# Loading the first pair early by hardware queues, and row tiles in batch 1, in a fused attention and feed-forward kernel

## Chip, cores and metric

One core of one Trainium2 chip. The metric is the time of one execution on the device, in microseconds (us); lower is better. Most executions of this kernel agree within 0.3%; the profiler's span, from the first to the last instruction, is some 2 us shorter than the time of the same run. The clock records of these traces show TensorE's clock as granted in two steps: full, or half. Where a run's mean granted clock is given, 0.99 in a span of 350 us means about 7 us at half clock.

## The reference

```python
def _attn_ref(q, k, v, f):                 # 8 batches, 8 heads, 576 tokens, head size 64; fp32
    scores = scale * np.matmul(q, k.transpose(0, 1, 3, 2))
    log_f = np.log(np.clip(f, 0.0001, 1.0))
    cum = np.cumsum(log_f, axis=-1)
    decay = cum[:, :, :, None] - cum[:, :, None, :]
    scores = np.where(causal, -1000000000.0, scores + decay)
    attn = np.exp(scores - np.max(scores, axis=-1, keepdims=True))
    attn = attn / (np.sum(attn, axis=-1, keepdims=True) + 1e-09)
    return np.matmul(attn, v)

def _moe_ref(x, w_in, w_out):              # 4608 tokens, 512 -> 2048 -> 512
    h = x @ w_in
    g = 0.5 * h * (1.0 + erf(h / sqrt(2)))
    return g @ w_out
# reference: x = attention, heads side by side; result = _moe_ref(x, w_in, w_out)
```

The decay is a ratio of exponentials, so the kernel does not add it to the scores: it weighs v (and a column of ones beside it) with exp(-cum) and divides by the weighed sum.

## The kernel before

Names: a *pair* is two heads, of which a batch has four; a *score tile* is one of four groups (t = 0 to 3) of a pair's scores; *AV* is the product of the exponentials with the weighed v, one per head; GEMM1 and GEMM2 are the two halves of the feed-forward. From batch 1 on, matmuls of GEMM2 of the batch before are put between the score tiles (*fills*). A GEMM2 step `"n"` is one full 128-row matmul; `"r"` is two *row tiles* of 64 rows that run beside each other into two PSUM banks, whose contents VectorE adds.

The start: loads, then the work on VectorE and ScalarE, then TensorE's order.

```python
    f_sb = consts.tile([BH, S], FP32)
    nc.sync.dma_start(f_sb, f.rearrange("b h s -> (b h) s"))
    load_qk_tokens(0, 0, 2)          # GpSimd queue: fp32 in memory, bf16 in SBUF
    load_qk_tokens(0, 2, 4)
    ident_bf = consts.tile([P, P], BF16)
    make_identity(nc, ident_bf)
    load_qk_tokens(0, 4, 6)
    nc.gpsimd.memset(v_sb[:, :, 0, 0:1], 0.0)
    load_v(0, 0, 4)
    ...                              # the masks key_of and after, on GpSimd
    nc.vector.tensor_scalar(f_sb, f_sb, 1e-4, 1.0, Alu.max, Alu.min)
    nc.scalar.activation(lf, f_sb, Act.Ln)
    nc.vector.memset(v_sb[0:D, :, 4, :], 0.0)
    nc.vector.tensor_tensor_scan(cum, ones, lf, 0.0, Alu.mult, Alu.add)
    nc.scalar.activation(wk, cum, Act.Exp, bias=cum[:, S // 2 : S // 2 + 1], scale=-1.0)
    ...
        warm_up(11)                  # matmuls on zeros
        transposes(0, o_psum, "o")   # q copied out by ScalarE, k by VectorE
        nc.vector.tensor_copy(key_of[D:P], key_of[0:D])
        nc.vector.tensor_copy(after[D:P], after[0:D])
        warm_up(2)
        scores(0, 0, 0)              # each ends in an exp on ScalarE
        scores(0, 0, 1)
        transposes(1, m_psum, "m")
        scores(0, 0, 2)
        ...                          # wk transposed to wT, which weighs v
```

Batch 1, and the plan of GEMM2 under batches 3 to 7:

```python
        for i in range(HP):          # pairs
            for t in range(4):
                scores(b, i, t)
                ...
                take(fill, FILL_1[i][t])          # 2 fills a tile in pairs 2 and 3
                if i and t in (1, 2):
                    av(i - 1, t - 1)
                if i > 1 and t == 0:
                    to_xT(b, i - 2, nc.vector.tensor_copy, o_psum, "o")
        to_xT(b, HP - 2, nc.vector.tensor_copy, o_psum, "o")
        av(HP - 1, 0)
        av(HP - 1, 1)
        gemm1_begin(1, both)

    PLAN = [
        (0, "o", 16 * "r"),
        (1, "m", 6 * "r" + "n" + 9 * "r"),
        (2, "m", "n" + 9 * "r" + "n" + 5 * "r"),
        (3, "s", 7 * "r" + 9 * "n"),
    ]
```

The softmax here doesn't subtract the row's maximum and nothing guards it: scores larger than these inputs give would overflow.

## Time and profile before

| | before |
|---|---|
| time, median | 348.35 us |
| span of the profiled run (its time: 347.52 us) | 345.7 us |
| TensorE busy | 95% |
| first score exp / first AV / first score of batch 1 | 8.60 / 17.12 / 39.67 us |
| batch 1 / batch 2 / each of batches 3 to 6 | 32.60 / 46.91 / 36.16 us |

A stage is read from the timeline, as the distance between the first instructions of two kinds. A timeline line gives start, duration, engine, source line, operation, output and inputs, shape and how many instructions were put together; in brackets how long the engine stood still before it, and what ended that.

### The profile page before, as it was taken

The page shows a single profiled execution, that of the slowest core. Times are in us where ns is not written, and L with a number is a line of the kernel's source. Part 1 is how long each engine was busy: PE and PEld are TensorE (multiplying, and loading weights), DVE is VectorE, ACT ScalarE, POOL GpSimd, SP SyncE. Part 2 cuts the span into 40 slices and gives each one's busy share as a digit, 9 for nine tenths or more (in the row PEclk, how much of TensorE's full clock was granted, in tenths as well). Part 3 has the DMA queues.
Part 4 walks back from the last instruction along what each step waited for, and adds up shares of the span by engine and source line. Part 5 has one row for each costly group of instructions (what it writes and reads, how often), then busy time and mean ns, then how long its engine had stood idle before and what let it go on. Part 6 is the DMA issues. An engine that isn't in the chain of part 4 may idle for free.

```text
span 345.7 us, 7895 instructions
## 1 busy us (share of the span) xinstructions
PE 328.3 (95%) x3187; PEld 173.7 (50%) x3227; DVE 188.1 (54%) x424; ACT 212.1 (61%) x296; POOL 125.1 (36%) x256
## 2 busy tenths in 40 slices
PE   7899999999999999999899989998999899999995
PEld 3674555445554455545554555445544554444443
DVE  5670456934367935795479647974597542020011
ACT  5976786773634787368746874687468765503600
POOL 8390673128418044533345333624261430000000
PEclk9999999999999999999999999999999999999999
DMA  8999999979992999488935995498900230011013
GB/s 116 176 171 194 202 178 147 170 149 161 222 183 100 138 202 176 81 119 167 219 89 81 134 211 137 74 161 190 170 30 2 69 83 30 2 61 61 0 35 89
DMA packets 99924, 43.03 MB, mean 124 GB/s; under 512 B 78704, under 2 KB 95344, under 8 KB 99888
## 3 DMA queue, kind: packets, MB, share of 16 engines
q1 hardware_dynamic: 82592, 28.37, 42.4%
q0 software_dynamic: 16896, 13.63, 26.9%
q8 instruction: 25, 0.41, 0.5%
q10 hardware_dynamic: 400, 0.52, 0.4%
q14 instruction: 11, 0.09, 0.1%
HBM read 36.85 MB, written 9.44 MB: 134 GB/s over the span
## 4 chain that ended last, share of the span: by engine, by line
PE 89%; DVE 4%; ACT 3%; issue 2%; POOL 2%; POOLq 0%; ACTq 0%; DVEq 0%
PE ps L375 35%; PE ps L466 25%; PE o L320 9%; PE ps L408 8%; PE s L289 8%; ACT e L299 2%; PE ps L501 2%; PE ps_x L353 1%; DVE ot L474 1%; PE ps_f L206 1%; DVE x L334 1%; POOL q L107 1%; POOL k L107 1%; DVE qT L213 0%; DVE kT L213 0%
## 5 line engine op out<-in xcount | busy, mean ns | idle before, releaser
L392 ACT ACTIVATE g<-ps 128x512 bf16<-128x512 f32 x144 | 85.3, 597 | 80.2 <-PE ps L375 80.2
L299 ACT ACTIVATE e<-s 128x896 bf16<-128x896 f32 (+2 forms) x128 | 101.0, 836 | 32.1 <-PE s L289 28.2
L375 PE MATMUL ps<-xT,w_in_sb 128*128 128x512 bf16 x497 | 111.4, 379 | 0.8
L466 PE MATMUL ps<-w_out_sb,g 64*128 64x512 bf16 (+1 forms) x736 | 104.0, 376 | 4.7 <-DVE ot L474 3.9
L375 PEld LDWEIGHTS <-w_in_sb 128*128 128x128 bf16 x576 | 56.0, 98 | 67.5 <-issue 1.8
L301 POOL TENSOR_SCALAR_AFFINE_SELECT e<-e 128x256 bf16<-128x256 bf16 (+1 forms) x135 | 49.5, 385 | 100.1 <-ACT e L299 99.9
L466 PEld LDWEIGHTS <-g 64*128 64x128 bf16 (+1 forms) x756 | 39.8, 94 | 40.4 <-issue 10.6
L244 DVE COPY qT<-tq 64x288 bf16<-64x288 bf16 x96 | 49.3, 514 | 1.4
L260 POOL TENSOR_TENSOR vw<-v_sb,wT 128x640 bf16<-128x640 f32 x31 | 39.6, 1279 | 24.7 <-DMA v_sb<-in_v_dram 24.5
L289 PE MATMUL s<-qT,kT 64*128 64x320 bf16 (+4 forms) x384 | 43.9, 277 | 3.3 <-ACT e L299 2.6
L320 PE MATMUL o<-vw,e 128*128 128x65 bf16 x960 | 36.8, 194 | 2.7 <-issue 2.4
L320 PEld LDWEIGHTS <-e 128*128 128x128 bf16 x960 | 34.8, 98 | 9.2 <-POOL e L301 4.1
L474 DVE COPY ot<-ps 128x512 f32<-128x512 f32 x26 | 17.9, 690 | 35.5 <-PE ps L466 35.5
L244 DVE COPY kT<-tk 64x288 bf16<-64x288 bf16 x96 | 33.0, 344 | 1.6
L334 DVE TENSOR_TENSOR x<-o,r 128x320 bf16<-128x320 f32 x64 | 31.5, 492 | 2.2
L417 DVE COPY ot<-ps 128x512 f32<-128x512 f32 (+2 forms) x9 | 5.7, 632 | 48.8 <-PE ps L408 31.9
L289 PEld LDWEIGHTS <-kT 64*128 64x128 bf16 x384 | 18.7, 94 | 22.6 <-issue 7.3
L333 DVE RECIPROCAL r<-o 128x5 f32<-128x5 f32 x64 | 12.2, 190 | 30.8 <-PE o L320 30.7
L408 PE MATMUL ps<-w_out_sb,g 128*128 128x512 bf16 (+2 forms) x142 | 27.9, 355 | 0.1
L408 PEld LDWEIGHTS <-g 128*128 128x128 bf16 x144 | 13.5, 98 | 14.5
L476 DVE TENSOR_TENSOR ot<-ot,ps 128x512 f32<-128x512 f32 x26 | 17.9, 687 | 1.2
L375 PE MATMUL ps<-tails,w_in_sb 128*128 128x512 bf16 x63 | 14.3, 377 | 0.1
(64 smaller groups left out, 148.2 us busy)
## 6 DMA issues: line engine op xcount, KB each, us to landing
out_dram<-ot SPq DMA_DIRECT2D x32, 256.0 KB, 2.3
v_sb<-in_v_dram SPq DMA_DIRECT2D x24, 256.0 KB, 5.7
q<-in_q_dram POOLq DMA_DIRECT2D x6, 576.0 KB, 6.2
k<-in_k_dram POOLq DMA_DIRECT2D x6, 576.0 KB, 8.2
v_sb<-in_v_dram SPq DMA_DIRECT2D x22, 128.0 KB, 5.3
w_in_sb<-in_moe_w_in_dram POOLq DMA_DIRECT2D x4, 512.0 KB, 7.0
w_out_sb<-in_moe_w_out_dram POOLq DMA_DIRECT2D x4, 512.0 KB, 8.4
q<-in_q_dram POOLq DMA_DIRECT2D x4, 144.0 KB, 4.5
```

Of the source, the lines that this page charges most:

```text
L244: nc.vector.tensor_copy(rows[:, odd], src[odd * D : (odd + 1) * D, 2 * i + h].rearrange("d j p -> d p j"),)
L260: eng.tensor_tensor(vw_of[b][:, hs, :, 0:D], v_sb[:, hs, :, :], w.unsqueeze(3).to_broadcast([P, 2, NBLK, D]), Alu.mult,)
L289: nc.tensor.matmul(to, *ab, start=half < 0, stop=half == 1 or not masked)
L299: nc.scalar.activation(et[:, :, z:c], st[:, :, z:c], Act.Exp, scale=scale)
L301: nc.gpsimd.affine_select(out=et[:, :, c0 + z : c0 + P], in_=et[:, :, c0 + z : c0 + P], compare_op=Alu.is_ge, fill=0.0, base=z, pattern=[[ ...
L320: nc.tensor.matmul(o[:, m, :], e_of[b, i, t][:, h, c : c + P], vw_of[b][:, 2 * i + h, n, :], start=(n == 0), stop=(n == m),)
L334: nc.vector.tensor_tensor(x_of[b, i][:, :, h, :], o[:, :, 0:D], r.unsqueeze(2).to_broadcast([P, NBLK, D]), Alu.mult,)
L375: nc.tensor.matmul(ps, w_in_sb[:, kt, ffb * P : (ffb + 1) * P], src[:, kt, 0:TC], start=(kt == 0), stop=(kt == n_dm - 1),)
L392: nc.scalar.activation(g_of[c][ffb], ps, Act.Gelu)
L408: nc.tensor.matmul(pss[ts][:, c0:c1], g_of[c][kt][:, ts * P : (ts + 1) * P], w_out_sb[:, kt, c0:c1], start=(kt == 0), stop=(kt == n_ff - 1),)
L466: nc.tensor.matmul(banks[r], g_of[c][kt][rows, ts * P : (ts + 1) * P], w_out_sb[rows, kt, :], start=kt == (steps.index("r") if r else 0), ...
L474: nc.vector.tensor_copy(ot, banks[1])
```

## The change

The intent, part by part. **Start**: q and k of the first pair come in fp32 by the hardware queues of SyncE and ScalarE instead of by GpSimd's, which frees GpSimd for the masks; VectorE casts them; the scan and exponential of the decay go behind the first scores and their copies, so that they do not hold these up. **Batch 1**: fills as row tiles, like the scores, so that TensorE changes its tiling less often; both AVs of a pair together; GEMM1's first matmuls ahead of the last AV; the mask of the last score tile added by TensorE instead of GpSimd. **Batch 2**: GEMM2's second half in row tiles as well, in another order. **Batches 3 to 7**: a full step is moved so that no block starts with a step that waits for a bank.

```diff
...
+    for src, dst, eng in zip((q, k), first, (nc.sync, nc.scalar)):
+        eng.dma_start(dst, src[0, 0:2].rearrange("h (p j) d -> p h (j d)", j=JT))
     nc.sync.dma_start(f_sb, f.rearrange("b h s -> (b h) s"))
-    load_qk_tokens(0, 0, 2)
-    load_qk_tokens(0, 2, 4)
     ident_bf = consts.tile([P, P], BF16)
     make_identity(nc, ident_bf)
+    load_qk_tokens(0, 2, 4)
     load_qk_tokens(0, 4, 6)
-    nc.gpsimd.memset(v_sb[:, :, 0, 0:1], 0.0)
-    load_v(0, 0, 4)                            # now behind the masks
...
+    for src, dst in zip(first, qk_of[0]):
+        nc.vector.tensor_copy(dst[:, 0:2], src)
     nc.vector.tensor_scalar(f_sb, f_sb, 1e-4, 1.0, Alu.max, Alu.min)
     nc.scalar.activation(lf, f_sb, Act.Ln)
-    nc.vector.tensor_tensor_scan(cum, ones, lf, 0.0, Alu.mult, Alu.add)
-    nc.scalar.activation(wk, cum, Act.Exp, bias=cum[:, S // 2 : S // 2 + 1], scale=-1.0)
+    table = consts.tile([1, 1], FP32)
+    nc.vector.memset(table, 0.0)
+    nc.scalar.activation(table, table, Act.Exp)
...
-        (1, "m", 6 * "r" + "n" + 9 * "r"),
-        (2, "m", "n" + 9 * "r" + "n" + 5 * "r"),
+        (1, "m", 6 * "r" + "n" + 8 * "r" + "n"),
+        (2, "m", 9 * "r" + "n" + 6 * "r"),
...                                             # gemm2_half: row tiles; each half block
...                                             # ends in a copy and an add on VectorE
-        warm_up(11)
+        warm_up(7)
         transposes(0, o_psum, "o")
...
         warm_up(2)
         scores(0, 0, 0)
+        nc.vector.tensor_tensor_scan(cum, ones, lf, 0.0, Alu.mult, Alu.add)
         scores(0, 0, 1)
+        nc.scalar.activation(
+            wk, cum, Act.Exp, bias=cum[:, S // 2 : S // 2 + 1], scale=-1.0
+        )
...
-    FILL = [[7, 6, 3, 3], [1, 3, 3, 3], [1, 3, 3, 3], [1, 3, 3, 3], [7]]
+    FILL = [[7, 6, 3, 3], [1, 3, 3, 2], [1, 3, 3, 3], [1, 3, 3, 3], [8]]
-    FILL_1 = [[0, 0, 0, 0], [0, 0, 0, 0], [2, 2, 2, 2], [2, 2, 2, 2]]
+    FILL_1 = [[0, 0, 0, 0], [0, 0, 0, 2], [2, 2, 2, 2], [2, 2, 2, 0]]
...
-                if i and t in (1, 2):
-                    av(i - 1, t - 1)
-                if i > 1 and t == 0:
+                if i == 1 and t in (1, 2):
+                    av(0, t - 1)
+                if i > 1 and t == 2:
                     to_xT(b, i - 2, nc.vector.tensor_copy, o_psum, "o")
+                    av(i - 1, 0)
+                    av(i - 1, 1)
...
-        to_xT(b, HP - 2, nc.vector.tensor_copy, o_psum, "o")
+        pss = [gemm1(1, ffb, (0, 1)) for ffb in range(2)]
         av(HP - 1, 0)
         av(HP - 1, 1)
...                                             # to_xT of pairs 2 and 3 among GEMM1's matmuls
```

## The prediction

> **What bounds the kernel now.** First the page: shares and the chain that ended last.
>
> ```profile
> PE 328.3 (95%) x3187; PEld 173.7 (50%) x3227; DVE 188.1 (54%) x424; ACT 212.1 (61%) x296; POOL 125.1 (36%) x256
> PE 89%; DVE 4%; ACT 3%; issue 2%; POOL 2%; POOLq 0%; ACTq 0%; DVEq 0%
> ```
>
> TensorE is on 89% of the chain. Matmul work itself does not change, so only time in which TensorE stands still can be won or lost. I looked for it in three stages, with the timeline and the chain in order of time.
>
> The start:
>
> ```profile
> f_sb<-in_f_dram SPq DMA_DIRECT2D x1, 144.0 KB, 2.6
> q<-in_q_dram POOLq DMA_DIRECT2D x4, 144.0 KB, 4.5
> ...
> 3.43 0.45 DVE L185 TENSOR_SCALAR f_sb<-f_sb 64x576 f32<-64x576 f32 x1 [1.55 <-DMA f_sb<-in_f_dram]
> 3.92 0.68 ACT L186 ACTIVATE f_sb<-f_sb 64x576 f32<-64x576 f32 x1 [1.83 <-DVE f_sb L185]
> 4.62 1.28 ACT L189 ACT_TABLE_LOAD   x1
> 6.02 0.78 ACT L189 ACTIVATE f_sb<-cum 64x576 f32<-64x576 f32 x1
> 6.70 0.62 ACT L213 COPY qT<-ps_f 128x576 bf16<-128x576 bf16 x1
> 8.60 5.72 ACT L299 ACTIVATE e<-s 128x896 bf16<-128x896 f32 x7 [1.28 <-PE s L289]
> ...
> 16.79 0.31 PE L289 MATMUL s<-qT,kT 64*128 64x320 bf16 x2 [0.25 <-ACT e L299]
> ```
>
> ScalarE runs log, table load, decay exp and the first qT copy in order, idles 1.28 us, then does score exps with almost no gap from 8.60. TensorE waits for those exps until 16.79; its first AV is at 17.12 and from there it is nearly full. So up to 17 us the bound is ScalarE, and the first exp's start sets it. That start was held 0.35 us at 8.16 by the copy of `after`, made late on GpSimd behind six load issues.
>
> Batch 1 (us 47 on):
>
> ```profile
> 47.07 0.37 PE L289 MATMUL s<-qT,kT 64*128 64x256 bf16 x4 [0.28 <-ACT e L299]
> 47.37 0.39 PE L501 MATMUL ps<-w_out_sb,g 128*128 128x512 bf16 x1
> 47.81 0.44 PE L353 MATMUL ps_x<-ident_bf,x 128*128 128x128 bf16 x5
> 48.19 0.34 PE L289 MATMUL s<-qT,kT 64*128 64x64 bf16 x4
> ```
>
> Scores are row tiles (64*128), the fill matmuls L501 full ones. Two score pairs of 256 and 192 columns stream for 0.19 us, to 47.26, and L501 starts 0.11 later; five transposes end near 48.08, and scores start 0.11 later. A round trip costs about 0.2 us.
>
> Batches 3 to 7, which repeat every 36.2 us:
>
> ```profile
> 128.72 0.45 PE ps L466 x4
> 129.19 0.70 DVE ot L474
> 130.31 0.95 PE o L320 x30
> ...
> PE ps L466 <- DVE ot L474: 3.9, 5, 0.8
> ```
>
> Five times (5 batches) a full step of the second GEMM waits 0.79 us for VectorE to copy a PSUM bank: in PLAN it is the first step of row block 2 and needs the banks of block 1 at once.
>
> **What the Trainium skill says.** "TensorEngine Tiling (Array Packing)", Key Properties: changing the tiling mode drains TensorE. The trace agrees, 0.11 us each way. "ScalarE: Activation LUTs", What ACT_TABLE_LOAD costs: about 1283 ns a load; the trace has 1283 ns. "VectorE: DVE Perf Modes", Mode 2x_2P: single-source fp32 operations in SBUF reach two elements a cycle. The clip of 576 took 453 ns, which is 300 at 0.96 GHz plus 153, so it agrees; no fp32 to bf16 cast of this size is in the trace. "DMA: Bandwidth & Descriptors", Specifications: hardware queues have a first byte about 0.4 us sooner than GpSimd's. Landing was 2.6 against 4.5 us here, a larger difference, part of which is queueing.
>
> **The start, part by part.** Removed: two load pairs ahead of GpSimd's masks. Before, GpSimd reached `key_of` at 5.92; it now has four issues of about 0.7 us ahead instead of six, so `after` is ready near 6.2 instead of 7.46, and no longer binds. Moved: q and k of the first pair come on SP and ACT from 0.81, f behind q. f alone landed at 3.43. q and k are each 288 KB in fp32, 576 together; 147 KB of f moved in about 0.7 us after its first packet at 2.73, and a packet of 2304 bytes took 93 ns on one of 16 engines (396 GB/s at best), so 590 KB need 1.5 us or more: landing near 4.2, f near 4.6. Added: two casts of 768, by the clip's rate 400 + 153 = 0.55 us each: 4.2 to 5.3. Only then the clip (0.45), log (0.68), table load (1.28), the tiny exp (0.2) and the qT copy (0.62) on ScalarE: 8.6. Scores to first exp take 0.78 without the mask wait (0.18 to the scores, 0.6 for them): first exp at about 9.3, against 8.60. The decay exp, which ran before 8.60, now sits after the second score exp, 0.74 more. Sum: ScalarE's chain is 0.7 + 0.74 = 1.4 us later. The diff has 7 warm-up matmuls instead of 11, ending at 1.26 + 7*0.43 = 4.3, which looks as if q was cast by then, 0.5 us sooner than my estimate. I choose **+0.8 us**.
>
> **Batch 1.** Removed: 16 fills in row tiles cost the same (a pair every 0.216 us), but 8 round trips in pairs 2 and 3 become 2: 6*0.2 = 1.2 us won. Two fills go in pair 1, where TensorE waited for exps (0.3 won), and a GpSimd mask of 0.41 us at the end leaves the path. Added: each half block ends in a copy and an add on VectorE (0.69 + 0.69), and counts put that end exactly at step 8 of pair 2 and step 16 of pair 3, just ahead of transpose copy and two AVs. The `o` pool has two buffers, so the second AV waits for the transpose copy: 0.12 + 1.34 + 0.49 = 2.0 us after the fill, while TensorE has only 0.1 + 0.27 + 0.48 = 0.85 of work. That is a new wait of about 1.1 us, twice: 2.2. At the end the transpose copy for pair 2 stands behind both normalizations of pair 3 on VectorE (2*0.65), with 0.43 us of GEMM to cover it: 0.8 lost, and the gelus come closer together. Sum: -1.2 - 0.3 - 0.4 + 2.2 + 0.8 = +1.1, and up to +2 with the gelus. I choose **+1.2 us**.
>
> **Batch 2.** Its first two blocks of 8 full steps become row tiles: two round trips, **-0.4 us**.
>
> **Batches 3 to 7.** Step 32 becomes the full step, accumulating in the bank it has. It starts at 129.08 instead of 129.93. The next block then needs that bank: copy 129.19 to 129.88, add to 130.57, while AV and scores fill to 130.54; nothing or 0.1 is lost. One fill fewer comes ahead and is done at the end (FILL 8 for 7): 0.216 is given back, since the score ahead is held by its exp anyway (end near 128.35). 0.85 - 0.1 - 0.2 = 0.55 to 0.63 per batch, five times: **-2.9 us**.
>
> Sum: 0.8 + 1.2 - 0.4 - 2.9 = -1.3, so 348.35 - 1.3 = 347.05, rounded 347.0.
>
> **Rivals.** (a) All parts are gains: casts are done at 4.3, the first exp comes before 8.0, and batch 1 keeps its 1.9 us. For it: counts look tuned on a chip. Against it: the VectorE and ScalarE order above. It would make start -0.5, batch 1 -1, total about 343.5 to 344.5. (b) Both new waits come in full (+1.4 or more, +2.0): 348.5. For it: every duration is from the trace. (c) The step moved in PLAN only moves the wait: the score or the next bank (VectorE's add) holds TensorE instead. Against it: the score's exp had ended by 128.35, and the add ends when TensorE arrives. It would leave -0.2 a batch and give about 349 to 350. (d) The early loads are hidden anyway, since AV needs v, which landed near 15.1; then the start changes by 0.
>
> **Range and chances.** (b) and my sum lie within 1.5 us, (a) 3 below, (c) alone 2 above. I hold 344.3 to 349.2 for 8 in 10. 2% is 7 us; the whole idle time found is about 3.9 + 1.9 + 1.3, all of which would have to be won: 0.02 faster, 0.97 within, 0.01 slower.
>
> **What would show it.** Right: the wait of L466 on DVE ot L474 is gone from the list of waits, the period of batches 3 to 7 falls from 36.2 to about 35.6; the first score exp lies at 8.8 to 9.4 and the decay exp two exps later; in batch 1, PE o waits about 1.1 us twice for an xT copy; gemm1 of batch 1 ends later relative to its start. Wrong: a first exp before 8.3; no such AV waits; a new wait of like size at the first step of row block 2.

## More of the kernel before

The prediction shows the views that I read beforehand. Here are two lines of TensorE's timeline of the kernel before, in its first 12 us, which it does not show and which matter later:

```profile
3.37 2.54 PE L195 MATMUL ps_w<-warm 128*128 128x512 bf16 x6
...
11.55 0.47 PE L206 MATMUL ps_f<-ident_bf,q 96*64 96x96 bf16 x10
```

The six warm-up matmuls take 0.42 us each. Ten transposes take 0.47 us. The first number is a matmul of 512 columns at half clock (in GEMM1 of this trace 41 matmuls of the same shape take 8.95 us, 0.22 each), the second is work at full clock; by the clock records of the trace TensorE has the full clock from about 5.6 us.

## The result, and the profile after

The changed kernel is correct and **slower**: 352.14 us median (351.94 to 353.63, 4 runs) against 348.33, ratio 1.0122, 95% interval 1.009 to 1.0154. Ratios here and below are the mean time of one kernel's fast runs over that of the other's of the same rounds, so not quite the ratio of the medians quoted. The predicted class (within 2%) held; the sign did not, and the time lies outside the range.

The span grew by 4.06 us. From the timelines of both kernels, in us:

| stage | before | after | difference | predicted |
|---|---|---|---|---|
| span's start to first score exp | 8.60 | 10.78 | +2.18 | } |
| first exp to first AV | 8.52 | 10.97 | +2.45 | } +0.8 for both |
| first AV to first score of batch 1 | 22.55 | 22.55 | 0.00 | 0 |
| batch 1 | 32.60 | 34.86 | +2.26 | +1.2 |
| batch 2 | 46.91 | 46.48 | -0.43 | -0.4 |
| batches 3 to 7 and the end | 226.48 | 224.08 | -2.40 | -2.9 |
| sum | 345.66 | 349.72 | +4.06 | -1.3 |

The page of the changed kernel, in the two lines that answer to the first two of the prediction:

```profile
PE 330.9 (95%) x3215; PEld 177.5 (51%) x3259; DVE 191.0 (55%) x432; ACT 211.5 (60%) x296; POOL 123.5 (35%) x253
PE 87%; ACT 5%; DVE 4%; issue 2%; DMA 1%; DVEq 0%; ACTq 0%
```

ScalarE's share of the chain rose from 3 to 5% and DMA entered it. Both belong to the start. First its issues (KB each, and us from issue to landing):

```profile
first_q<-in_q_dram SPq DMA_DIRECT2D x1, 288.0 KB, 4.4
...
f_sb<-in_f_dram SPq DMA_DIRECT2D x1, 144.0 KB, 5.0
```

f took 2.6 us before and takes 5.0 behind q. q takes 4.4. By GpSimd's queue the same q took 3.7 in the kernel before (4.5 is the median of its four loads of q); the 144 KB listed there are what lands as bf16, read from the same fp32 in memory. VectorE's timeline:

```profile
5.27 0.56 DVE L191 CAST q<-first_q 96x768 bf16<-96x768 f32 x1 [3.39 <-DMA first_q<-in_q_dram]
5.75 0.87 DVE L191 CAST k<-first_k 96x768 bf16<-96x768 f32 x1
```

The first cast starts at 5.27, not at 4.2. ScalarE's timeline then is the following; the lines with L307 are score exps:

```profile
7.10 0.68 ACT L193 ACTIVATE f_sb<-f_sb 64x576 f32<-64x576 f32 x1 [4.54 <-DVE f_sb L192]
...
9.21 0.61 ACT L221 COPY qT<-ps_f 128x576 bf16<-128x576 bf16 x1
10.78 1.62 ACT L307 ACTIVATE e<-s 128x896 bf16<-128x896 f32 x2 [0.97 <-PE s L297]
12.29 0.77 ACT L558 ACTIVATE f_sb<-cum 64x576 f32<-64x576 f32 x1
...
14.43 1.61 ACT L307 ACTIVATE e<-s 128x640 bf16<-128x640 f32 x2 [0.44 <-PE s L297]
16.88 1.62 ACT L307 ACTIVATE e<-s 128x768 bf16<-128x768 f32 x2 [0.84 <-PE s L297]
```

The kernel before had seven exps in one stretch of 5.72 us. Here the decay exp sits between them, and ScalarE waits for TensorE's scores at 14.43 and 16.88. TensorE's timeline says why:

```profile
5.88 0.86 PE L214 MATMUL ps_f<-ident_bf,q 96*64 96x96 bf16 x12 [1.45 <-DVE q L191]
...
9.87 0.40 PE L297 MATMUL s<-qT,kT 64*128 64x256 bf16 x2 [1.37 <-ACT qT L221]
...
15.01 0.70 PE L214 MATMUL ps_f<-ident_bf,q 96*64 96x96 bf16 x10
```

Ten transposes take 0.70 us where they took 0.47. TensorE is at half clock. The page does not tell this: the view by windows, whose last columns are granted clock, DMA share and GB/s, has for the changed kernel

```profile
5.00:11.00 6.00, 3.75 (x44) 2.42 (x44) 4.71 (x9) 2.90 (x5) 3.39 (x12) 1.00 1.27 212
```

that is, 1.00. The clock records of the trace begin with the first grant of the full clock, and what lies before is counted as full. They put that grant at about 5.6 us in the kernel before and about 18.9 us in the changed one (aligned with the span by matmul durations and the mean clock, good to some 0.3 us; expectations below that were written earlier use an alignment some 0.5 us later).

In batch 1, TensorE's timeline and then VectorE's, after the change:

```profile
56.20 0.63 PE L328 MATMUL o<-vw,e 128*128 128x65 bf16 x15 [1.09 <-DVE xT L364]
...
61.52 0.64 PE L328 MATMUL o<-vw,e 128*128 128x65 bf16 x15 [1.09 <-DVE xT L364]
```

```profile
55.06 0.69 DVE L522 TENSOR_TENSOR ot<-ot,ps 128x512 f32<-128x512 f32 x1
55.66 0.48 DVE L364 COPY xT<-ps_x 128x640 bf16<-128x640 bf16 x1
```

The AV waits twice for the copy of xT, which stands behind the add of a GEMM2 block, as predicted, to 0.01 us. In batches 3 to 7 the wait of L466 on VectorE's `ot` (3.9 us) is gone. The list of waits (us in total, times, longest) of the changed kernel has instead

```profile
PE o L328 <- DVE ot L484: 0.8, 5, 0.2
```

### The profile page after: what moved, and what is told of

Read it like the earlier page. It is cut to its first block, busy times and chain, and to the rows that moved or that the text cites. A ratio compares the mean times of both kernels' runs of the same rounds, so it can differ in the third digit from the quotient of the medians.

```text
span 349.7 us, 7972 instructions
## 1 busy us (share of the span) xinstructions
PE 330.9 (95%) x3215; PEld 177.5 (51%) x3259; DVE 191.0 (55%) x432; ACT 211.5 (60%) x296; POOL 123.5 (35%) x253
## 4 chain that ended last, share of the span: by engine, by line
PE 87%; ACT 5%; DVE 4%; issue 2%; DMA 1%; DVEq 0%; ACTq 0%
PE ps L383 34%; PE ps L474 24%; PE o L328 9%; PE s L297 8%; PE ps L416 8%; ACT e L307 3%; PE ps L505 2%; PE ps_f L214 1%; DMA first_q<-in_q_dram 1%; PE ps_x L361 1%; DVE x L342 1%; ACT g L400 1%; DVE xT L364 1%; DVE ot L517 0%; DVE ot L522 0%
## 5 line engine op out<-in xcount | busy, mean ns | idle before, releaser
L307 ACT ACTIVATE e<-s 128x896 bf16<-128x896 f32 (+2 forms) x128 | 100.9, 836 | 32.4 <-PE s L297 30.7
L309 POOL TENSOR_SCALAR_AFFINE_SELECT e<-e 128x256 bf16<-128x256 bf16 (+1 forms) x134 | 48.8, 383 | 103.7 <-ACT e L307 103.3
L474 PEld LDWEIGHTS <-g 64*128 64x128 bf16 (+1 forms) x756 | 41.4, 94 | 40.2 <-issue 11.9
L297 PE MATMUL s<-qT,kT 64*128 64x320 bf16 (+4 forms) x384 | 47.5, 285 | 4.2 <-ACT e L307 2.4
L297 PEld LDWEIGHTS <-kT 64*128 64x128 bf16 x384 | 20.4, 95 | 24.5 <-issue 10.1
L373 POOL COPY tails<-xT 128x256 bf16<-128x256 bf16 x8 | 3.2, 399 | 39.8 <-DVE xT L364 34.1
```

Source lines behind the costliest of these rows:

```text
L297: nc.tensor.matmul(to, *ab, start=half < 0, stop=half == 1 or not masked)
L307: nc.scalar.activation(et[:, :, z:c], st[:, :, z:c], Act.Exp, scale=scale)
L309: nc.gpsimd.affine_select(out=et[:, :, c0 + z : c0 + P], in_=et[:, :, c0 + z : c0 + P], compare_op=Alu.is_ge, fill=0.0, base=z, pattern=[[ ...
L474: nc.tensor.matmul(banks[r], g_of[c][kt][rows, ts * P : (ts + 1) * P], w_out_sb[rows, kt, :], start=kt == (steps.index("r") if r else 0), ...
```

## The experiments

Fifteen kernels ran in four calls of up to four; each call has its own runs of the kernel before, with medians of 347.71, 348.24, 348.19 and 348.10. All results were correct. Times are medians of four runs; the interval is of the ratio to the kernel before. Times are compared with care, since the runs of the kernel before scatter too (347.45 to 352.18). So do traces: the five that start as the kernel before does (`before`, `start_undone`, `plan_only`, `xt_early`, `best`) have their first AV at 16.91 to 17.97 us, the later ones with TensorE waiting up to 0.6 us for loads of later pairs. A shift of the first AV by less than about 1 us in one trace therefore shows nothing by itself.

### Which part costs: the start undone, the plan alone

`start_undone` is the changed kernel with the whole start of before.

```diff
-    (fp32 loads on SyncE and ScalarE, casts, tiny exp; scan and decay exp among the scores; warm_up(7))
+    (GpSimd loads, scan and decay exp ahead of the scores; warm_up(11))
```

> The changed kernel with its start put back as it was before (loads, warm-ups, decay scan), all else kept. In the two traces the first matmul of the first GEMM moved from 24.27 to 28.89 us, and batch 1's first score by the same 4.63. If the start alone made that loss, this takes 352.1 - 4.6 = 347.5 us and its first GEMM begins at 24.3. If the start cost what the prediction gave it (0.8 us), it takes 351.3.

Measured: 347.53 us, ratio 0.9992 (0.9972 to 1.0012). First exp 8.24, first AV 17.39. The start as a whole costs the 4.6 us that the traces show: 352.14 - 347.53 (4.5 by the ratios).

`plan_only` is the kernel before with the new `PLAN` and `FILL` alone.

> The kernel before with only PLAN and FILL changed (batches 3 to 7). The prediction's step: the 0.79 us wait of the second GEMM for VectorE's copy goes, 2.9 us in five batches: 345.4. From the trace after: those batches and the tail end 2.2 us closer: 346.1. If the wait only moved to the next bank (rival c), 348 to 350.

Measured: 345.73 us, ratio 0.9938 (0.992 to 0.9955): 2.0 us faster. The period of batches 3 to 6 is 35.67 against 36.16. This part is a gain by itself.

### Is it the warm-ups?

`before_7warm`: the kernel before with `warm_up(7)` in place of `warm_up(11)`.

> The kernel before with 7 warm-up matmuls instead of 11: one number changed. Theory clock: TensorE stays at half speed over the first scores as in the changed kernel, and the time rises by 1.5 to 2 us to about 350. Rival: transposes wait for q anyway until 5.8 us, so the warm-ups are hidden and the time stays 348.3.

Measured: 348.12 us, ratio 1.0007 (0.9989 to 1.0024). The full clock came at about 10 us instead of 5.6, and the first AV at 17.72 instead of 17.12. The 4.6 us more at half clock cost at most 0.6 us in the trace, no more than such traces scatter, and nothing measurable in time. So the mere number 7 is not the loss. Also, in this run the transposes of the q that came by GpSimd's queue began at 4.97 us: earlier than the cast of the q that came by the hardware queue.

`after_warm`: the changed kernel with more warm-ups, to lift the clock.

```diff
-        warm_up(7)
+        warm_up(10)
...
-        warm_up(2)
+        warm_up(9)
```

> The changed kernel with 10 warm-up matmuls instead of 7 ahead of the first transposes and 9 instead of 2 behind them, nothing else. Theory clock: TensorE ran at half speed until about 19 us because 7 warm-ups are too few to bring its clock up; then score matmuls and transposes between 10 and 19 us take half as long (24 transposes in 0.74 instead of 1.27 us), ScalarE's exps close up, the first AV comes at about 19.9 instead of 21.75, and the time is about 350.3. Rival (only the late operands and the decay exp delay ScalarE's chain, the slow matmuls are hidden beneath it): 352.1, unchanged.

Measured: 352.12 us, ratio 1.0122 (1.0103 to 1.014), no gain. The exps did close up (five in one stretch from 12.70). But VectorE's weighing of pair 0's v, which now ran beside GpSimd's, became slow, and the AV waited for it. VectorE's timeline and TensorE's:

```profile
17.57 2.85 DVE L268 TENSOR_TENSOR vw<-v_sb,wT 128x640 bf16<-128x640 f32 x1
```

```profile
20.60 0.65 PE L328 MATMUL o<-vw,e 128*128 128x65 bf16 x15 [0.85 <-DVE vw L274]
```

In other runs this operation takes 0.82 to 0.96 us. In this one, the clock then fell to half again for 3.4 us from about 21.1.

`after_warm_vw`: the same, with the weighing ahead of `scores(0, 1, 0)`.

```diff
+        weigh_v(0, 0, nc.vector)
         scores(0, 1, 0)
...
-        weigh_v(0, 0, nc.vector)
```

> As after_warm, and VectorE's weighing of v for the first pair stands ahead of the score of pair 1 instead of behind all four. In after_warm the exps had closed up (last score before the first AV at 19.35 us instead of 21.42), but that weighing took 2.85 us instead of 0.84 beside GpSimd's weighings, the first AV waited for it until 20.60, and the clock fell again from 21.7 to 25.1. Theory clock: with the weighing out of the way the first AV comes at about 19.7 and the time is about 350.1. Rival (the clock is worth nothing): 352.1 again.

Measured: 353.60 us, ratio 1.0128 (1.0065 to 1.019). A miss: the weighing took 0.83, but the small cast behind it, again beside a weighing of GpSimd's, took 1.27 us (0.18 in the kernel before), the copies of the next pair's q came late, TensorE stood still for 1.36 us, and the clock was lost for 6.8 us.

`f_first`: the same, with f loaded ahead of q and k and clipped ahead of the casts.

> after_warm_vw with f loaded ahead of q on its queue and the clip ahead of the two casts on VectorE, so that log and table load on ScalarE no longer stand behind the casts. Theory serial chain: the first score exp comes at about 9.3 us instead of 10.5, and the time is 1.2 us less than after_warm_vw, about 348.9. Rival (the late landing of q and k alone sets the first exp): no less than after_warm_vw.

Measured: 353.31 us (350.68 to 356.39), ratio 1.0088 (0.999 to 1.0186), and the profiled run was slow (more than 1.5% above the kernel's fastest). Inconclusive: the nine warm-ups ran at half clock and held the first scores until 12.24 us by themselves. In that trace the log began 0.74 us earlier than in `after_warm_vw` (6.33 against 7.07), but q, now behind f, was cast so late that its transposes began 1.67 us later (7.52 against 5.85).

`after_warm_pool`: `after_warm`, with pair 0's v weighed on GpSimd.

```diff
-        weigh_v(0, 0, nc.vector)
+        weigh_v(0, 0)
```

> The run with 10 and 9 warm-up matmuls (TensorE at the full clock for the first scores), with one thing changed: pair 0's values are weighed by GpSimd and no longer by VectorE, whose weighing took 2.85 us there and held the first attend up by 0.85 us. Theory (the start's loss beyond the late q and k is TensorE's half clock, and the first attempt to cure it only failed on the slow weighing, after which the clock fell again): the first attend starts at about 19.7 us without a wait for VectorE, the clock records stay at full to the end, and the time is about 350.1 us, 2 us under the 352.1 of the run it comes from. Rival (the clock is not worth anything here, or GpSimd's weighing is as late): first attend at 20.6 us or later, 352 us.

Measured: 351.36 us, ratio 1.0071 (1.0036 to 1.0106). The clock stayed full from before the first scores (from about 10.4 us), and the first AV came 9.16 us after the first exp instead of 10.97. ScalarE's timeline has the decay exp of 0.77 us between these two lines, and no gap behind it:

```profile
11.62 1.62 ACT L307 ACTIVATE e<-s 128x896 bf16<-128x896 f32 x2 [1.51 <-PE s L297]
...
13.79 4.19 ACT L307 ACTIVATE e<-s 128x896 bf16<-128x896 f32 x5
```

The first exp itself came late, at 11.62, since the nine warm-ups, most of them at half clock, ran until 11.05. By the medians 0.8 us of the expected 2 was gained; the rest was lost to the remedy.

### The loads alone, and the clock by itself

`loads_only`: the changed kernel with scan and decay exp back ahead of the scores, and `warm_up(11)`.

```diff
-    table = consts.tile([1, 1], FP32)
-    nc.vector.memset(table, 0.0)
-    nc.scalar.activation(table, table, Act.Exp)
+    nc.vector.tensor_tensor_scan(cum, ones, lf, 0.0, Alu.mult, Alu.add)
+    nc.scalar.activation(wk, cum, Act.Exp, bias=cum[:, S // 2 : S // 2 + 1], scale=-1.0)
...
-        warm_up(7)
+        warm_up(11)
```

> The changed kernel with the decay scan and its exponential put back ahead of the first scores, as in the kernel before, and 11 warm-up matmuls; what stays of the start's change is the first pair's q and k in fp32 by hardware queues, cast by VectorE. Against the run that has the whole start of before (347.5 us). Theory (the late landing and the casts cost about 2.5 us, the half clock comes on top): first exponential at about 11.2 us, first attend at about 19.7 us, about 350.2 us if the clock records show full clock in the first scores, about 352 if they show half. Rival (my prediction's step: the loads cost 0.8 us in all): 348.3 us.

Measured: 350.73 us, ratio 1.0067 (1.0015 to 1.012). First exp 11.03, first AV 21.31. TensorE had the full clock early, stood still while it waited for qT (TensorE's timeline), and then ran at half clock, so ScalarE's exps have gaps again (ScalarE's timeline):

```profile
10.46 0.28 PE L296 MATMUL s<-qT,kT 64*128 64x256 bf16 x2 [2.78 <-ACT qT L220]
```

```profile
13.12 1.66 ACT L306 ACTIVATE e<-s 128x896 bf16<-128x896 f32 x2 [0.47 <-PE s L296]
...
16.77 1.62 ACT L306 ACTIVATE e<-s 128x768 bf16<-128x768 f32 x2 [0.85 <-PE s L296]
```

`loads_warm`: `loads_only` with `warm_up(10)` and `warm_up(7)`, which fill that stretch, and pair 0's v on GpSimd.

> The run with the late loads alone (decay scan and its exponential ahead of the first scores; it measured 350.7 us, with half clock from 11.5 to 18.3 us after an idle stretch of TensorE of 2.8 us), with 10 and 7 warm-up matmuls that fill this stretch and pair 0's values weighed by GpSimd. If the half clock was what kept it from 350 us: first exponential at 11.0 us, first attend at 19.6 us (8.5 later, as in the kernel before, since no decay exponential lies between), time about 349 us. What is left over the 347.5 us of the run with the old start is then the landing and the casts. Rival (the clock matters little): 350.7 us, first attend at 21 us or later.

Measured: 349.42 us, ratio 1.0046 (1.0018 to 1.0074). First exp 11.03, first AV 19.55: 8.52 later, exactly as in the kernel before. ScalarE's timeline shows the exps closed:

```profile
11.03 5.72 ACT L306 ACTIVATE e<-s 128x896 bf16<-128x896 f32 x7 [0.63 <-PE s L296]
16.96 5.44 ACT L306 ACTIVATE e<-s 128x640 bf16<-128x640 f32 x7 [0.20 <-PE s L296]
```

Both kernels have their first exp at 11.03; the first AVs differ by 1.76 us and the medians by 1.3. In time this pair proves little, because the intervals overlap; the trace is the evidence. (The weighing moved too, but in neither kernel did the first AV wait for it.) Of the four runs of `loads_warm`, three had mean clock 1.00 and took 348.96 to 349.42; the fourth had 0.99 and took 351.14.

`before_cold`: the test from the other side, the kernel before almost without warm-ups.

```diff
-        warm_up(11)
+        warm_up(1)
...
-        warm_up(2)
```

> The kernel before with 1 warm-up matmul in place of 11 and 2, nothing else changed: TensorE's half clock by itself. Theory: the clock comes up only at 12 us or later, gaps open between the first exponentials, the first attend comes at 18.5 us or later instead of 17.1, and the time is 1.5 to 2 us over before, about 350 us. Rival (as the run with 7 for 11 showed, cold scores cost at most 0.4 us, since ScalarE bounds the stage): first attend at 17.6 us or earlier and 348.5 us.

Measured: 349.60 us, ratio 1.0041 (1.0025 to 1.0058). The full clock came at about 15.5 us, the first exp at 8.48, as before, and the first AV at 19.34, 2.2 us later than before (0.34 of it a wait for the weighed v). The profiled run was the slowest of the four by 0.9 us; 0.6 us of its span lies in batch 2, not in the start. ScalarE's timeline has the gaps of the changed kernel:

```profile
10.78 1.67 ACT L299 ACTIVATE e<-s 128x896 bf16<-128x896 f32 x2 [0.68 <-PE s L289]
...
14.43 1.62 ACT L299 ACTIVATE e<-s 128x768 bf16<-128x768 f32 x2 [0.84 <-PE s L289]
```

So half clock makes these gaps without any other part of the change. `before_7warm` did not show it because its clock rose at 10 us, when the first exps still had scores in hand; read from these traces, the loss comes from about 11 to 18 us, where each exp needs the transposes of another pair.

`warm6`: the changed kernel with `warm_up(10)` and `warm_up(6)`, pair 0's v on GpSimd.

> The changed kernel with 10 and 6 warm-up matmuls (7 and 2 there; 10 and 9 in the earlier runs, where the nine ran until 11.05 us and so held the first scores up by 0.85 us themselves) and pair 0's values weighed by GpSimd. Theory (half clock costs 1.8 us between the first exponential and the first attend, and nothing else stands in the way of taking it back): first exponential at 10.8 us, first attend 9.2 us later at 20.0, clock full from before the first scores; time 0.8 us under that of the run with nine, about 350.4 us, 1.7 under the changed kernel. Rival (the time does not follow the trace's start): 351.4 us, as with nine, or more.

Measured: 351.68 us, ratio 1.01 (1.007 to 1.013). The first exp came at 10.35, earlier than expected; but the clock, full at first, was at half from about 11.9 to 18.7 in the profiled run, and the first AV came at 21.39. TensorE's timeline has two waits here, one for qT and one that only the late decay exp makes, in the middle of the scores:

```profile
9.78 0.28 PE L297 MATMUL s<-qT,kT 64*128 64x256 bf16 x2 [1.24 <-ACT qT L221]
...
12.77 0.55 PE L565 MATMUL psw<-ident_fp,f_sb 64*128 64x64 f32 x3 [0.99 <-ACT f_sb L558]
```

The second wait, from 11.78 on, had scarcely begun when the clock fell, so it can hardly be what lost it. The four runs split by clock: 350.32 at 1.00 and 351.57 at 0.998, against 351.78 and 352.81 at 0.99. The fastest is the 350.4 that I expected of a full clock, but whether the clock holds differs from run to run. As a remedy it fails.

`before_wk`: the kernel before with scan and decay exp behind the first scores, without the loads.

```diff
-    nc.vector.tensor_tensor_scan(cum, ones, lf, 0.0, Alu.mult, Alu.add)
-    nc.scalar.activation(wk, cum, Act.Exp, bias=cum[:, S // 2 : S // 2 + 1], scale=-1.0)
+    (the tiny exp here; scan behind scores(0, 0, 0), decay exp behind scores(0, 0, 1))
```

> The kernel before with only the decay scan and its exp moved behind the first scores, and the Exp table loaded by a tiny exp, as in the changed kernel. The prediction's step: the decay exp of 0.74 to 0.78 us now stands between score exps on the chain that sets the first AV, so +0.7: 348.4 beside 347.7. Rival (it fills an idle moment of ScalarE, as the change intends): 347.7 or less.

Measured: 348.39 us beside 348.24, ratio 0.9968 (0.99 to 1.0037); the time separates nothing. In the trace the first exp came 0.15 us earlier and the first AV 0.7 later (17.82), which is within the scatter of such traces. What the trace does show is the term itself: from the start of the decay exp to the next score exp it is 0.67 us.

### Batch 1

`xt_early`: `start_undone` with the transposes of pair i - 2 back at tile 0.

```diff
-                if i > 1 and t == 2:
+                if i > 1 and t == 0:
                     to_xT(b, i - 2, nc.vector.tensor_copy, o_psum, "o")
+                if i > 1 and t == 2:
                     av(i - 1, 0)
```

> start_undone (347.5 us) with the transpose of the pair before last in batch 1 put back to the start of a pair (t 0), the two AVs staying together. The prediction's step: the second AV waits 1.09 us twice for the buffer that the transpose holds until VectorE has done copy and add of the fill; both waits go, one round trip of tiling modes (0.2) comes back in each pair: 345.7. Rival (batch 1's loss lies in its tail, the first GEMM with the transposes behind the normalizations): 347.5.

Measured: 346.81 us, ratio 0.9938 (0.9867 to 1.001). In the trace batch 1 takes 32.69 against 34.57 in `start_undone`, 1.88 less, and both waits of the AV are gone. What is left of VectorE's copy of xT in the waits is at the tail:

```profile
PE ps L375 <- DVE xT L356: 0.6, 1, 0.6
```

So, in the trace, the two waits are the loss in batch 1. Without them it takes as long as in the kernel before (32.60), not less: the row tiles and the other order win nothing there on balance. In time the expected 345.7 was missed, and the interval does not separate the run from `start_undone`.

`best` adds to `xt_early` the transposes of pair 2 between the last pair's first attend and its normalization, and puts GEMM1 matmuls ahead of the last transposes.

> The start of the kernel before, the changed plan of batches 3 to 7 and of batch 2, and batch 1 as row tiles with the transposes of each pair put ahead of the next attend, so that VectorE's copy of xT is not behind a normalization; for the last pair they lie between the last attend and its normalization. Theory: batch 1 gives back its 2.3 us and the plan keeps its 2.4, so about 344.5 us (0.988 to 0.991 of the kernel before). Rival (batch 1 as row tiles is worth nothing even without its waits): as the run with the plan alone, 345.7 us.

Measured: 346.41 us (345.33 to 347.63), ratio 0.9942 (0.9897 to 0.9987). The expected 344.5 was missed, and the rival held. Batch 1 takes 32.60. In the trace, of its fastest run, the span is 343.1, against 343.5 for `plan_only`; in time it cannot be told from `plan_only`, which is the simpler edit. Both beat the kernel before by about 0.6%.

`best_masks`: `best`, with the masks and first v loads ahead of the q and k loads of heads 4 to 7 on GpSimd.

> The run of the same call called best, with the masks and the first v loads put ahead of the q and k loads of heads 4 to 8 on GpSimd's queue. If the decay chain waits for the masks in the start: first exponential at 8.1 us and 0.4 us less than best. Rival: the transposes of the third pair wait for their q instead, and the time is that of best or up to 0.5 us more.

Measured: 350.81 us, ratio 1.0052 (0.9999 to 1.0105), 4.4 us over `best`. The rival held, and worse than it said: the first exp stayed at 8.39, and TensorE waited for q and k of pairs 2 and 3:

```profile
13.85 0.56 PE L206 MATMUL ps_f<-ident_bf,q 96*64 96x96 bf16 x12 [0.56 <-DMA q<-in_q_dram]
14.93 0.56 PE L206 MATMUL ps_f<-ident_bf,k 96*64 96x96 bf16 x12 [0.52 <-DMA k<-in_k_dram]
```

These waits, and with them the first AV, cost 1.5 us against `best`; another 1.7 us lie in batch 2, where the AVs wait twice, 1.3 us in all, for masks on GpSimd. The profiled run, at full clock, took 348.6; the other three had mean clocks of 0.985 to 0.99 and took 350.7 to 352.4. That waits of this size lose the clock is likely from this, but here they were not separated.

## Why the prediction was wrong

Predicted -1.3 us, measured +3.8 (348.33 to 352.14).

**The start is the step that failed**: "I choose +0.8 us". It cost +4.63 in the trace and 4.6 in time. The prediction's own sign for it, a first score exp "at 8.8 to 9.4", failed at 10.78. Three terms:

- *The first exp, +2.18 where the text had "about 9.3, against 8.60".* I had q and k "landing near 4.2" from bytes over bandwidth; q was cast from 5.27, because its load took 4.4 us from issue to landing. The wrong term is the rate. The trace's packet records have q's packets from 1.9 to 4.4 us and k's from 2.3 to 4.8: 590 KB in 2.9 us, about 200 GB/s where the sum took 396. The number was at hand: f's 147 KB moved from 2.2 to 3.0 us in the kernel before (not from the "2.73" that I read), 184 GB/s, and at that rate 590 KB need 3.2 us. The next error is small: the two casts ran to 6.62, 1.35 us in all for twice "0.55" (the first took 0.56, the second 0.87). Everything behind them (clip, log, table load, qT copy) ran as written, so the qT copy ended at 9.82 for "8.6". From there to the first exp it took 0.96 us, 0.3 more than at full clock (0.63 in `loads_only`). I also discounted my own sum of 1.4 to 0.8 because of the diff's seven warm-ups, "which looks as if q was cast by then". A count in the source is not a measurement.
- *The decay exp, +0.6.* Written as 0.74; with a full clock (`after_warm_pool`) the stretch from first exp to first AV is 9.16 against 8.52. This term was right. What the move won in return is about the same at full clock: the first exp of `warm6` is 0.68 us ahead of that of `loads_only`, which has the decay exp in its old place. In the changed kernel, whose first scores run at half clock, it is only 0.25 us ahead.
- *TensorE at half clock, +1.8.* Missing altogether. 10.97 - 9.16 = 1.81 against `after_warm_pool`, 10.28 - 8.52 = 1.76 between `loads_only` and `loads_warm`, and 10.86 - 8.52 = 2.34 (0.34 of it another wait) between `before_cold` and before. Shown in both directions in the traces, and in time by `before_cold` (1.5 us, its interval clear of 1). The warm-up matmuls ran out at 4.4 us, q came at 5.3, and TensorE had pauses of 1.45 and 1.37 us, so its clock rose only at about 18.9. The Trainium skill, "TensorE: Matmul & The Clock Gate", Part 1, has this: half rate until a window of about 3.4 us has been busy. The traces agree: the records of half clock between two of full clock last 3.41 or 6.83 us. Counted back from 18.9 in steps of 3.41 us, TensorE was busy for 2.61, 2.62, 2.20 and 3.26 us of the four steps from 1.8 to 15.5, and 15.5 to 18.9 is the first step that it filled; in the kernel before, it filled 2.1 to 5.5 and had the grant then. I had read the number of warm-ups as a hint at the landing of q, and not asked what they do to the clock.

2.18 + 0.64 + 1.81 = 4.63, by construction: the last two split the difference of first exp to first AV. Of the rivals, (b), "Both new waits come in full", came nearest in mechanism, at 348.5; it lacked the clock and the later landing too. (c) has the nearer number (349 to 350), but its mechanism did not happen, as said below; nor did (a), a first exp "before 8.0", or (d), a start that changes by 0.

**Batch 1** had the mechanism and the wrong size. The "new wait of about 1.1 us, twice: 2.2" was exact (1.09 twice), and `xt_early` gave 1.88 back by removing it. The wrong term is the gain, "-1.2 - 0.3 - 0.4" = -1.9: measured up to the end of the last AV, and with the GEMM1 matmuls that were moved ahead of it (0.65 us) taken out, batch 1 is 1.24 us longer, so the gain was 2.18 - 1.24 = 0.9. The tail lost 1.0 from there to batch 2 where "0.8" stood. Which of the three gains fell short was not separated.

**Batch 2**: -0.43 for "-0.4". **Batches 3 to 7**: the wait went as described; -0.49 a batch for "0.55 to 0.63", and the AV waits 0.16 us for VectorE's add where I had "nothing or 0.1". With the prediction's other two terms, 0.85 - 0.16 - 0.2 = 0.49; these two were not measured apart. In time, `plan_only` is 2.0 us faster. Rival (c), that the wait only moves, is refuted.

**What stays open**: why the early loads moved at some 200 GB/s (no run changed their size or split), and exactly which pauses make the clock fall. `after_warm_pool` and `warm6` have the same wait of 1.0 us for the decay exp; one kept the clock in its profiled run, the other lost it. What the traces show is how much idle time it took. Laid out in steps of 3.41 us from the first grant, in the first 30 us of all profiled runs, the clock fell after steps in which TensorE was busy for 0.72 us (`loads_only`), 1.24 and 1.97 (`f_first`), 1.70 (`after_warm`), 1.89 (`after_warm_vw`) and 2.00 (`warm6`), and held after every step with 2.15 or more. In `warm6` that step is 8.5 to 11.9, with the wait for qT in it; `after_warm_pool` has no such wait after its grant, and at least 2.36 us busy. It is no sharp limit: later in the kernels single steps with just under 2 us held, as the one at 53.0 us in the changed kernel (1.97).

## What to carry to other kernels

Before moving an early load, write down when the first real matmul will run and whether TensorE is busy from the warm-ups up to it: a pause of one or two microseconds there can cost more at half clock than the pause itself (1.24 us in `warm6`, with 1.88 us more from the first exp to the first AV than in `after_warm_pool`). Read the clock from the duration of matmuls of one shape, since a mean granted clock of 1.00 does not cover the time before the first grant. In a change of several parts, run each part alone: here the edit of `PLAN` and `FILL` carried the whole gain (345.73 us), and the rest hid it.

## What the Trainium skill lacked or had wrong

- "TensorE: Matmul & The Clock Gate", Part 1 names an idle window of about 3.4 us as what brings half rate back. Here the clock was lost with no single pause over 2.78 us (`loads_only`) and, in `warm6`, with none over 1.24 us, after a step of 3.41 us of which TensorE was busy for 2.00. A later part of the page tells of short idle stretches that do this too, but gives no figure for how much is enough. The page warns that the window runs freely; that the same kernel keeps the clock in one run and loses it in the next is what the four runs of `warm6` show (1.00 to 0.99).
- No page says that a mean granted clock leaves out the start: the changed kernel has a mean of 1.000 and ran its first scores, until about 18.9 us, at half clock.
- "DMA: Bandwidth & Descriptors", Specifications gives the hardware queues a first byte 0.4 us sooner. That is not contradicted here, but for loads early in a kernel it does not decide: the first pair's q took 4.4 us by a hardware queue (288 KB, with k and f beside it) and 3.7 us by GpSimd's (144 KB landing as bf16).
